# Five buffers instead of three for float64 weight blocks, loads four blocks ahead, and another choice of the blocks that are converted early

## The chip, the cores and the metric

The kernel runs on one core of one Trainium2 chip. The metric is the time of one execution in microseconds (us), the median of several runs; smaller is better. The engines are named as the profile names them: PE is TensorE (PEld its weight loads), DVE VectorE, ACT ScalarE, POOL GpSimd, and SP the engine whose queue issues every DMA of this kernel.

## What is computed

Sigmoid attention over 8 batches of 12 heads (448 tokens, head size 64), then a block that adds the real part of a two-dimensional Fourier transform, normalizes, and applies a feed-forward layer with a residual. All inputs are float32 but the two weight matrices, which are float64.

```python
def _attn_ref(q, k, v):
    scores = scale * np.matmul(q, k.transpose(0, 1, 3, 2)) - np.log(S)
    attn = 1.0 / (1.0 + np.exp(-scores))
    return np.matmul(attn, v).astype(np.float32)

def _moe_ref(x, w_ch1, w_ch2):
    X = np.fft.fft(np.fft.fft(x, axis=1), axis=2)
    u = x + np.real(X).astype(np.float32)
    mu = np.mean(u, axis=-1, keepdims=True)
    var = np.mean((u - mu) ** 2, axis=-1, keepdims=True)
    un = (u - mu) / np.sqrt(var + 1e-06)
    ch = np.maximum(un @ w_ch1, 0.0) @ w_ch2
    return (u + ch).astype(np.float32)
```

Here x is the output of attention, 3584 tokens of 768 numbers; w_ch1 is 768 x 3072 and w_ch2 3072 x 768.

## The kernel before

**Weights.** Each matrix is cut into 24 blocks, (0, f) of the first and (1, f) of the second, 128 partitions of 768 float64 words, 768 KB. Float64 words are handled as pairs of 32-bit integers. Three things happen to a block. Its largest magnitude is taken over the upper halves of its words (weight_max, L289: one DVE instruction, `wmax<-wr`); the scales of the matrices come out of all 48 maxima. It is converted to float32 (to_float32, L295: ACT at L300, DVE at L302, L306 and L308). And it is split into a high and a low float16 half with the scale (prep_w, L464: ACT at L491, DVE at L495).

**Attention** (L618 to L638) runs in steps t of one tile of scores: TQ = 168 steps, emitted in pairs. A pair emits what earlier pairs left for ACT and DVE (flush), the maxima that are due (`when_w`), the scores of two tiles (PE at L155 and L148, sigmoid on ACT at L159), the entries of the table `extra` for these steps, the loads that are due (`loads_w`), the products with v of two tiles LAG = 2 steps back (L176), and some units of the Fourier mixing of an earlier batch (mix_units, L208). Units write PSUM banks (`psd`, `pss`, `psx`), of which two are used at a time here; ACT or DVE reads a bank an emitted pair later (A, Q on ACT; sm, df and u on DVE, L240 and L259), and only then is it free for another unit. POOL casts queries and keys (L131), DVE makes their remainders ql and kl (L136).

The maximum of block n = 24 i + f stands at step 22 + n * 114 // 48, a block every 2.4 steps. Loads of blocks (weight_load, L282) go into three buffers called wr, and load n + 2 is emitted one step behind the maximum of block n, or two where block n - 1 is one of the set `ready`. The ten blocks of `ready` are converted as well (convert, L311) in three parts, at the step of the maximum and two and four steps behind it, into one of three buffers of float32 words (tag wt), and stored to t_dram (L318), 384 KB each. They are (0, 7), (0, 11), ... (0, 23) and (1, 5), (1, 9), ... (1, 21).

**Order.** `pin` (L529) binds every engine's instructions, SP's DMAs among them, to the order in which the code emits them, so an engine that waits holds up all that stands behind it.

**Towards the feed-forward.** The feed-forward takes blocks in the list `order`: (0, 0), (0, 1), (0, 2), (1, 0), (0, 3), (1, 1), (0, 4), (1, 2) and so on. Place k in it is a slot. prep_step (L498) emits a slot in four parts: loads of up to four places ahead, as far as buffers are free by `loadable`; the conversion on ACT of place k + 1 and the high half of place k - 1, whose float32 words are stored to t_dram; the conversion on DVE of place k; the low half of place k - 1. A block of `ready` is loaded from t_dram (L474), half as many bytes, and needs neither conversion nor store. Besides the three buffers wr two more, called spare, take the places from 8 on with k % 5 of 3 or 4.

A loop (L724 to L741) emits the last units of the mixing. It emits parts of slots too: of MIX_STEP rounds in turn the first four take one part each. Then come the chunks of 512 tokens. The first two are plain (NPLAIN): for each f an up-projection (PE at L669, result psh), its evacuation (evac, L672: hh on ACT, hl on DVE), two slots if the chunk is the first, and the down-projection of the f before (L688). The last five chunks run from a recombined copy of the weights, w_dram, with products in another form (L910, L961); the kept float16 blocks are written there from f = KEEP_FROM = 14 of the first chunk on (L784).

Of the kernel before, what the change touches and what calls it, by code (L numbers as in the profile page):

```python
# [11 lines left out]
I32 = mybir.dt.int32  # L12
# [11 lines left out]
DM = 768  # L24
# [3 lines left out]
NFC = DF // 128  # L28
# [4 lines left out]
BT = NT7 * NG  # L33
FOLDS = ((1, 2, 4, 5, 9, 9), (2, 2, 4, 4, 5, 5), (0, 0, 1, 1, 2, 2))
NPRE = 3
NW1 = 17
NW2 = 3
LEAD = 4
LNT = 2
UNIT_US = 0.66  # L40
MIX_UP = 8
MIX_STEP = 7

UN_SCALE = 1.0
TW = 512
# [15 lines left out]
def spectral_attention_ffn(tc, q, k, v, w1, w2, cd, cs, ident_in, out):  # L61
# [8 lines left out]
    with ExitStack() as top:  # L70
# [12 lines left out]
        wpre = top.enter_context(tc.tile_pool(name="wpre", bufs=1))  # L83
        w1p = wpre.tile([128, NPRE, 2, NCC, 128], F16, tag="w1p", name="w1p")
        w1h, w1l = [w1p[:, f, 0] for f in range(NPRE)], [w1p[:, f, 1] for f in range(NPRE)]
        w2h, w2l = [], []
# [3 lines left out]
        if True:  # L90
# [3 lines left out]
            io = att_ctx.enter_context(tc.tile_pool(name="io", bufs=2))  # L94
# [185 lines left out]
            wtile = {}  # L280

            def weight_load(n):  # L282
                if n < 2 * NFC:
                    i, f = divmod(n, NFC)
                    wtile[n] = t = wpre.tile([128, DM, 2], I32, tag="wr", name="wr", bufs=3)
                    nc.sync.dma_start(
                        t.rearrange("p n w -> p (n w)"), (w1, w2)[i][:, f * 2 * DM:(f + 1) * 2 * DM])

# [156 lines left out]

            prep = {}

            ready = {(i, f) for i in range(2) for f in range(7 - 2 * i, NFC, 4)}
            order = [(0, f) for f in range(NPRE)]
            for f in range(NFC):  # L450
                order += [(1, f)] + [(0, f + NPRE)] * (f + NPRE < NFC)

            spare = []

# [74 lines left out]
            def pin():  # L529

                ins = nc.cur_bb.bb.instructions
                for i in ins[seen[0]:]:
                    e = str(i.engine)
                    if e in seen[1]:
                        tc.add_manual_dep(
                            i, seen[1][e].name,
                            mybir.DependencyInfo(mybir.DependencyClass.NoSync, mybir.DependencyReason.DATA),
                            reason="order")
                    seen[1][e] = i
                seen[0] = len(ins)  # L540
# [18 lines left out]
            TQ = NT7 * GG  # L559
            TP = max(TQ - 4 * NPRE - 10, 1)  # L560
            TM = TP - 10
# [3 lines left out]
            loads_w = {}  # L565
            for t, x in when_w.items():
                for n in x:
                    loads_w.setdefault(t + (2 if divmod(n - 1, NFC) in ready else 1), []).append(n + 2)
            extra = {}

            def at(t, fn):
                extra.setdefault(t, []).append(fn)
# [24 lines left out]
                    at(4 + 4 * c + 2 * par, lambda c=c, par=par: nc.sync.dma_start(cd_sb[:, c, par], cd[:, c, par]))  # L597
            at(12, lambda: nc.sync.dma_start(cs_sb, cs))
            at(14, lambda: nc.sync.dma_start(ident, ident_in))
            at(16, lambda: weight_load(0))  # L600
            at(18, lambda: weight_load(1))
            nc.vector.memset(ones, 1.0)
            for n in range(5):
                at(TP - 8 + 2 * ((n + 1) // 2), lambda n=n: weight_scales(n))
            prepped = set()
            for e in range(NPRE + 2):
                for n, d in enumerate((-2, 2, 4, 6, 8, 10)):
                    t = TP + 4 * e + d
# [9 lines left out]
            for t in range(0, TQ + LAG + 4, 2):  # L618
                flush(sp_next)
                flush(act_next)  # L620
                flush(dve_next)
                for i in range(t, t + 2):
                    for n in when_w.get(i, ()):
                        weight_max(n)
                for i in range(t, t + 2):
                    if i < TQ:
                        scores(i)
                for i in range(t, t + 2):
                    for fn in extra.pop(i, ()):
                        fn()  # L630
                    for n in loads_w.get(i, ()):
                        weight_load(n)
                for i in range(t - LAG, t - LAG + 2):
                    if 0 <= i < TQ:
                        values(i)
                mix_some(2 * UNIT_US)
                pin()
# [5 lines left out]
        with ExitStack() as fast, ExitStack() as st, ExitStack() as early:  # L643
# [6 lines left out]
            def blocks(pool, i, fs):  # L650
                for f in fs:
                    t = pool.tile([128, 2, DM], F16, name=f"w{i + 1}_{f}")
                    both[i, f] = t
                    for n, x in enumerate(((w1h, w1l), (w2h, w2l))[i]):
                        x.append(t[:, n].rearrange("p (c f) -> p c f", f=128) if i == 0 else t[:, n])

            both = {(0, f): w1p[:, f].rearrange("p n c f -> p n (c f)") for f in range(NPRE)}
            blocks(wp, 0, range(NPRE, NW1))
            blocks(wp, 1, range(NW2))
# [64 lines left out]
            while units or act_next or dve_next or sp_next:  # L724
# [6 lines left out]
                if len(units) < MIX_UP and m < NCC:  # L731
                    up_proj(0, 1, range(m, m + 1))
                    m += 1
                n = step % MIX_STEP
                if n < 4 and slot < NPRE + 2 * NW2 and (n or len(units) > 3):
# [11 lines left out]
            ps_o = st.enter_context(tc.tile_pool(name="ps_o", bufs=1, space=PSUM, side="right"))  # L747
            blocks(wp2, 0, range(NW1, NFC))
            blocks(wp2, 1, range(NW2, NFC))
# [86 lines left out]
            for j in range(NFC):  # L836
                f = 1 + j - (j > 4) - (j > 8) - (j > 12) - (j > 16)
# [4 lines left out]
            for n, x in enumerate(kept):  # L842
                at = KEEP_FROM + n // 3 if n < 3 * (NFC - KEEP_FROM) else NFC + n - 3 * (NFC - KEEP_FROM)
# [6 lines left out]
            for c in range(NPLAIN):  # L850
                for f in range(NFC):
# [27 lines left out]
                    pin()  # L879
                    if c == NPLAIN - 1 and f == NW1 + 1:  # L880
                        early.close()
# [133 lines left out]
            for c in range(NPLAIN + 1, NCK):  # L1015
                t = (c - NPLAIN - 1) * NQ * NU
# [3 lines left out]
            for g in range(NGR):  # L1020
                t = g * NU
# [84 lines left out]
```

## Time and profile before

| | us |
|---|---|
| time before, median of 3 runs | 1670.48 (1667.25 to 1673.29) |
| the profiled execution's own time | 1672.77 |
| its span in the trace | 1670.9 |
| PE busy in it | 1621.0 (97%) |
| DVE busy | 1237.0 (74%) |
| ACT busy | 607.9 (36%) |
| POOL busy | 202.3 (12%) |

Attention ends at about 415 us of the span, the mixing loop at 440, the first plain chunk at about 635. The trace holds for every instruction its start, its duration and, where its engine sat idle before it, how long and whom it waited for. Durations of matmuls are modelled, so the starts tell more than the sums. A DMA's row on SP (SPq) is its issue, not its transfer. Groups of instructions read: line, engine, operation, output <- input, shapes, count, busy us, mean ns of one, idle us before them and what ended it.

### The profile page before, as it was taken

To read this page: it belongs to the slowest core of one execution; us is meant where nothing else is said; L and a number is where in the kernel's file an instruction comes from. 1 tells how busy PE (TensorE), PEld (TensorE's weight loads), DVE (VectorE), ACT (ScalarE), POOL (GpSimd) and SP (SyncE) were. 2 spreads that over 40 slices of the span, in tenths; PEclk is the share of its full clock that TensorE was granted. 3 is DMA by queue.
4 is the path that set the end of the run, shared out by engine and by line. 5 is a ranking of instruction groups with operands and counts; after the bars stand their busy time and mean duration, and the time that the engine had idled before them with its cause. 6 is when DMAs were issued, how large, how long until landed. Compare 5 with 4: busy or idle time off the path is not lost.

```text
span 1670.9 us, 27354 instructions
## 1 busy us (share of the span) xinstructions
PE 1621.0 (97%) x10913; PEld 1046.6 (63%) x10913; DVE 1237.0 (74%) x2393; ACT 607.9 (36%) x791; POOL 202.3 (12%) x219
## 2 busy tenths in 40 slices
PE   9989998999799999998999999999999999999997
PEld 4545454545455555554677777777777777777774
DVE  3456577767588756787568888888888888887777
ACT  5545454555254432333143323332333233323221
POOL 4535543455000000000000000000000000000000
PEclk9999999999899999999999999999999999999998
DMA  6665868756587985887675656565756565656561
GB/s 224 243 244 211 283 233 308 238 140 212 204 268 256 343 304 189 286 293 261 223 279 217 233 199 260 216 233 199 261 216 233 199 261 215 233 199 241 207 256 39
DMA packets 109185, 390.99 MB, mean 234 GB/s; under 512 B 22801, under 2 KB 48642, under 8 KB 93698
## 3 DMA queue, kind: packets, MB, share of 16 engines
q1 hardware_dynamic: 109058, 389.26, 64.9%
q8 instruction: 85, 1.39, 0.3%
q14 instruction: 42, 0.34, 0.1%
HBM read 312.15 MB, written 73.92 MB: 231 GB/s over the span
## 4 chain that ended last, share of the span: by engine, by line
PE 48%; DVE 2%; DMA 0%; ACT 0%; issue 0%; ACTq 0%; DVEq 0%
PE psf L910 24%; PE pso L961 23%; PE pst L808 1%; DVE acc L970 1%; DVE acc L985 0%; DMA ws<-w_dram 0%; DVE ur L989 0%; DVE F L916 0%; DVE H L916 0%; ACT H L945 0%; ACT F L935 0%; DVE X L916 0%; DVEq L916 0%; ACTq L945 0%; ACTq L935 0%
## 5 line engine op out<-in xcount | busy, mean ns | idle before, releaser
L961 PE MATMUL pso<-ws,H 128*128 128x384 f16 x2520 | 422.6, 326 | 0.9 <-DVE H L916 0.8
L910 PE MATMUL psf<-ut,ws 128*128 128x256 f16 x3780 | 422.1, 273 | 1.1 <-DVE ur L709 1.1
L910 PEld LDWEIGHTS <-ws 128*128 128x128 f16 x3780 | 369.8, 98 | 50.4 <-issue 1.4
L961 PEld LDWEIGHTS <-H 128*128 128x128 f16 x2520 | 246.4, 98 | 155.7 <-DVE H L916 1.1
L970 DVE TENSOR_TENSOR acc<-pso,acc 128x384 f32<-128x384 f32 x350 | 181.5, 548 | 19.1 <-PE pso L961 19.1
L159 ACT ACTIVATE a<-sc 128x900 f32<-128x900 f32 x168 | 147.6, 919 | 129.2 <-PE sc L155 112.7
L688 PE MATMUL po<-w,hh 128*128 128x512 f16 (+1 forms) x768 | 179.2, 328 | 7.3 <-ACT w L491 6.8
L935 ACT ACTIVATE F<-F 128x1024 f32<-128x1024 f32 x60 | 63.4, 1056 | 331.8 <-DVE F L916 331.8
L669 PE MATMUL psh<-ut,w 128*128 128x512 f16 x756 | 170.0, 379 | 2.0 <-ACT U L809 2.0
L916 DVE TENSOR_TENSOR H<-F,H 128x1024 f16<-128x1024 f32 x120 | 129.4, 1086 | 46.9 <-ACT H L945 46.9
L176 PE MATMUL av<-a,vr 128*64 128x450 f32 (+1 forms) x768 | 153.1, 568 | 0.0
L916 DVE TENSOR_TENSOR F<-X,psf 128x256 f32<-128x256 f32 x240 | 97.8, 417 | 51.5 <-PE psf L910 48.5
L945 ACT ACTIVATE H<-F 128x1792 f16<-128x1792 f32 x60 | 101.8, 1697 | 88.8 <-DVE F L916 88.8
L669 PEld LDWEIGHTS <-w 128*128 128x128 f16 x756 | 74.0, 98 | 91.4 <-issue 2.3
L688 PE MATMUL po<-w,hl 128*128 128x512 f16 (+1 forms) x384 | 126.1, 328 | 1.4 <-DVE hl L677 1.4
L688 PEld LDWEIGHTS <-hh 128*128 128x128 f16 x768 | 75.5, 98 | 56.3 <-issue 8.7
L916 DVE TENSOR_TENSOR F<-F 128x256 f32<-128x256 f32 x240 | 91.1, 421 | 17.2 <-ACT F L935 12.9
L291 DVE TENSOR_REDUCE wmax<-wr 128x1 f32<-128x768 f32 x48 | 45.5, 949 | 71.6 <-DMA wr<-w_in 71.6
L677 DVE SCALAR_TENSOR_TENSOR hl<-psh,hh 128x512 f16<-128x512 f32 x48 | 33.0, 687 | 80.6 <-ACT hh L676 80.6
L176 PEld LDWEIGHTS av<-a,vr 128*64 128x64 f32 (+1 forms) x768 | 39.5, 136 | 76.6 <-issue 73.6
L916 DVE TENSOR_TENSOR X<-X,psf 128x256 f32<-128x256 f32 x180 | 74.6, 414 | 16.5 <-PE psf L910 11.3
L218 PEld LDWEIGHTS psd<-cd_sb,xp 128*113 128x113 f32 x384 | 62.3, 180 | 25.1 <-issue 17.6
(108 smaller groups left out, 1748.4 us busy)
## 6 DMA issues: line engine op xcount, KB each, us to landing
ws<-w_dram SPq DMA_DIRECT2D x120, 1344.0 KB, 6.6
wr<-w_in SPq DMA_DIRECT2D x74, 768.0 KB, 7.4
cb<-t_dram SPq DMA_DIRECT2D x24, 768.0 KB, 5.3
t_dram<-wt SPq DMA_DIRECT2D x38, 384.0 KB, 5.9
qr<-q_in SPq DMA_DIRECT2D x48, 225.0 KB, 5.3
kr<-k_in SPq DMA_DIRECT2D x48, 224.0 KB, 6.4
vr<-v_in SPq DMA_DIRECT2D x24, 448.0 KB, 3.2
spare<-w_in SPq DMA_DIRECT2D x12, 768.0 KB, 5.6
```

The source lines that it names most:

```text
L159: nc.scalar.activation(a, ps[:, :, :SQ], AF.Sigmoid, bias=-math.log(S), scale=1.0 / math.sqrt(D))
L176: nc.tensor.matmul(avp[pr][j * D:(j + 1) * D, :SQ], vr[k, v0:v0 + D], a[k, j], start=(c == 3 * pr), stop=(c == 3 + 3 * pr))
L218: nc.tensor.matmul(ps[:HM, par * 193:par * 193 + 193], xp[:, kp ^ c, c, par, p], cd_sb[:, c, par, p], start=(p == par == 0), stop=(p == 2 ...
L291: nc.vector.tensor_reduce(out=wmax[:, i, f:f + 1], in_=wtile[n][:, :, 1].bitcast(F32), op=ALU.max, axis=AX.X, apply_absolute_value=True)
L669: nc.tensor.matmul(hs[c, f], l[f][:, m], r[:, m], start=(m == n == 0), stop=(m == NCC - 1 and n == 2))
L688: nc.tensor.matmul(po[n][:, at:at + hi - lo], l[:, cols], r[f][:, lo:hi], start=(f == 0 and m == 0 and at == 0), stop=(f == NFC - 1 and m ...
L910: nc.tensor.matmul(ps[:, :TH], w[:, x, a, m * 128:(m + 1) * 128], ut[y][:, b, m], start=(m == n == 0), stop=(m == n == 2))
L916: nc.vector.tensor_tensor(out=o, in0=x, in1=y, op=op)
L935: nc.scalar.activation(F[:, 0:4], F[:, 0:4], AF.Relu)
L945: nc.scalar.activation(hts[P][:, 0], F[:, 1:8], AF.Copy)
L961: nc.tensor.matmul(ps[:, :384], H[:, x, a, tp * 128:(tp + 1) * 128], w[:, y, b], start=(j == n == 0), stop=(j == 1 and n == 2))
L970: later(0, lambda: nc.vector.tensor_tensor(out=to, in0=ps[:, :384], in1=to, op=ALU.add))
```

## The change

Loads of float64 blocks during attention get two more buffers: block n uses one of the three wr buffers where n % 5 is 0, 1 or 2, and otherwise one of two buffers of the pool of attention's inputs, io, which is given back when attention ends. Load n + 4 stands where load n + 2 stood, and the first four go out at steps 16 to 19 in place of two at 16 and 18. The ten blocks that are converted in attention are now the places 3 to 12 of `order`: (1, 0), (0, 3), (1, 1), (0, 4), (1, 2), (0, 5), (1, 3), (0, 6), (1, 4), (0, 7). MIX_STEP goes from 7 to 4.

```diff
 NPRE = 3
+NREADY = 10
...
-MIX_STEP = 7
+MIX_STEP = 4
...
-                    wtile[n] = t = wpre.tile([128, DM, 2], I32, tag="wr", name="wr", bufs=3)
+                    wtile[n] = t = (io, wpre)[n % 5 < 3].tile(
+                        [128, DM, 2], I32, tag="wr", name="wr", bufs=2 + (n % 5 < 3))
...
-            ready = {(i, f) for i in range(2) for f in range(7 - 2 * i, NFC, 4)}
             order = [(0, f) for f in range(NPRE)]
             for f in range(NFC):
                 order += [(1, f)] + [(0, f + NPRE)] * (f + NPRE < NFC)
+
+            ready = set(order[NPRE:NPRE + NREADY])
...
-                    loads_w.setdefault(t + (2 if divmod(n - 1, NFC) in ready else 1), []).append(n + 2)
+                    loads_w.setdefault(t + (2 if divmod(n - 1, NFC) in ready else 1), []).append(n + 4)
...
-            at(16, lambda: weight_load(0))
-            at(18, lambda: weight_load(1))
+            for n in range(4):
+                at(16 + n, lambda n=n: weight_load(n))
```

Lines of the changed kernel are one to three higher. On SP, where the first blocks are loaded in attention (wr are blocks of weights, kr, qr and vr keys, queries and values), before:

```order
L286 DMA wr<-w_in 128x1536
L120 DMA kr<-k_in 128x448
L121 DMA qr<-q_in 128x450
L286 DMA wr<-w_in 128x1536
L120 DMA kr<-k_in 128x448
L121 DMA qr<-q_in 128x450
L127 DMA vr<-v_in 128x896
L286 DMA wr<-w_in 128x1536
```

and now:

```order
L288 DMA wr<-w_in 128x1536 x2
L121 DMA kr<-k_in 128x448
L122 DMA qr<-q_in 128x450
L288 DMA wr<-w_in 128x1536 x2
L121 DMA kr<-k_in 128x448
L122 DMA qr<-q_in 128x450
L128 DMA vr<-v_in 128x896
L288 DMA wr<-w_in 128x1536
```

Two more loads of blocks have gone out by the same key and query loads, and from there on each load is two blocks further ahead.

On DVE, in attention from step 80 on (u reads a bank of the mixing, ql and kl are remainders, a t with a number is a block's float32 words), before:

```order
L259 TENSOR_TENSOR u<-psx,df 113x384
L291 TENSOR_REDUCE wmax<-wr 128x1
L259 TENSOR_TENSOR u<-psx,sm 113x384 x2
L136 TENSOR_TENSOR ql<-qr,qh 128x450
L136 TENSOR_TENSOR kl<-kr,kh 128x384
L259 TENSOR_TENSOR u<-psx,df 113x384
L259 TENSOR_TENSOR u<-psx,df 112x384
```

and now:

```order
L260 TENSOR_TENSOR u<-psx,df 113x384
L293 TENSOR_REDUCE wmax<-wr 128x1
L308 SCALAR_TENSOR_TENSOR t_1802<-wr,t_1802 128x768
L310 SCALAR_TENSOR_TENSOR t_1802<-wr,t_1802 128x768
L304 TENSOR_SCALAR t_1846<-t_1846 128x768
L260 TENSOR_TENSOR u<-psx,sm 113x384 x2
L308 SCALAR_TENSOR_TENSOR t_1846<-wr,t_1846 128x768
L310 SCALAR_TENSOR_TENSOR t_1846<-wr,t_1846 128x768
L304 TENSOR_SCALAR t_1901<-t_1901 128x768
L137 TENSOR_TENSOR ql<-qr,qh 128x450
L137 TENSOR_TENSOR kl<-kr,kh 128x384
L260 TENSOR_TENSOR u<-psx,df 113x384
```

Six instructions of the conversions of (1, 0) to (1, 2) stand between reads of banks now; two more conversions follow in the next steps.

On ACT, from the evacuation of up-projection (0, 1) to that of (0, 2) (hh is the evacuation, w_0 to w_5 with a number are high halves, wt is a conversion), before:

```order
L676 ACTIVATE hh<-psh 128x512
L300 ACTIVATE wt<-wr 128x768
L491 ACTIVATE w_3_4086<-wt,wsc 128x768
L300 ACTIVATE wt<-wr 128x768
L491 ACTIVATE w_1_4101<-wt,wsc 128x768
L300 ACTIVATE wt<-spare 128x768
L491 ACTIVATE w_4_4087<-wt,wsc 128x768
L300 ACTIVATE wt<-spare 128x768
L491 ACTIVATE w_2_4102<-wt,wsc 128x768
L676 ACTIVATE hh<-psh 128x512
```

and now:

```order
L494 ACTIVATE w_3_4083<-wr,wsc 128x768
L494 ACTIVATE w_1_4098<-wr,wsc 128x768
L679 ACTIVATE hh<-psh 128x512
L494 ACTIVATE w_4_4084<-wr,wsc 128x768
L494 ACTIVATE w_2_4099<-wr,wsc 128x768
L494 ACTIVATE w_5_4085<-spare,wsc 128x768
L494 ACTIVATE w_3_4267<-spare,wsc 128x768
L679 ACTIVATE hh<-psh 128x512
```

The high halves of (0, 3) and (1, 1) (w_3_4083 and w_1_4098) have moved ahead of the evacuation, two more blocks are reached by the next, and no conversion stands among them.

## Prediction

> **What bounds the kernel now.** I read first the busy time by stage, then the waits of TensorE (PE), then the instructions of the engine that each of them names, and last the rows of the step at which the feed-forward begins. By stage (us; busy time of PE, its weight loads, DVE, ACT, POOL; granted clock, DMA share, GB/s):
>
> ```profile
> 0.00:440.00 440.00, 415.03 (x2512) 222.47 (x2513) 275.29 (x447) 218.97 (x294) 202.27 (x219) 0.98 0.67 228
> 440.00:464.00 24.00, 16.69 (x78) 8.15 (x77) 15.08 (x20) 8.44 (x11) 0.00 (x0) 0.79 0.81 276
> 464.00:560.00 96.00, 96.00 (x517) 50.30 (x515) 80.33 (x100) 46.89 (x60) 0.00 (x0) 1.00 0.81 268
> 560.00:608.00 48.00, 48.00 (x262) 25.54 (x261) 37.54 (x46) 21.99 (x28) 0.00 (x0) 1.00 0.94 341
> 840.00:1640.00 800.00, 799.15 (x6148) 602.82 (x6146) 652.59 (x1482) 245.09 (x325) 0.00 (x0) 1.00 0.60 225
> ```
>
> PE is the bound everywhere: full from 464 to 608 and, from 840 on, idle for 0.85 us in 800. The change touches only what lies before 608. There PE idles 440 - 415.03 = 25.0 us in attention and 24 - 16.69 = 7.3 us where the feed-forward begins, and the clock under 1.00 says that more is lost than the idle time. The largest stops in attention (start, duration, line, in brackets idle time before and whom PE waited for):
>
> ```profile
> 100.78 1.05 PE L252 MATMUL psx<-ident,xT 128*112 128x128 f32 x6 [3.62 <-DVE u L259]
> 104.34 0.74 PE L155 MATMUL sc<-qh,kl 64*128 64x450 f32 x2 [0.59 <-DVE kl L136]
> 200.07 1.05 PE L252 MATMUL psx<-ident,xT 128*113 128x128 f32 x6 [3.00 <-DVE u L259]
> 262.31 0.74 PE L155 MATMUL sc<-ql,kh 64*128 64x450 f32 x2 [6.07 <-DVE ql L136]
> 322.36 0.47 PE L155 MATMUL sc<-ql,kh 64*128 64x450 f32 x2 [2.17 <-DVE ql L136]
> ```
>
> They name DVE, but DVE was not busy: just before each it stood in order behind a maximum over a weight block that had not landed. The waits of DVE sum this up (total, times, longest):
>
> ```profile
> 98.04 0.95 DVE L291 TENSOR_REDUCE wmax<-wr 128x1 f32<-128x768 f32 x1 [6.13 <-DMA wr<-w_in]
> 198.60 0.95 DVE L291 TENSOR_REDUCE wmax<-wr 128x1 f32<-128x768 f32 x1 [5.26 <-DMA wr<-w_in]
> 260.76 0.95 DVE L291 TENSOR_REDUCE wmax<-wr 128x1 f32<-128x768 f32 x1 [6.50 <-DMA wr<-w_in]
> 315.05 0.95 DVE L291 TENSOR_REDUCE wmax<-wr 128x1 f32<-128x768 f32 x1 [1.73 <-DMA wr<-w_in]
> DVE wmax L291 <- DMA wr<-w_in: 71.6, 25, 8.1
> ```
>
> The second stop, where the feed-forward begins, is PE waiting for the high half of block (1,1), which ACT makes late because its conversion started late (below it SP's issues, a stretch of 8 us with its DMA rate at the end, and two rows of the page: KB each, median us to landing):
>
> ```profile
> 455.20 0.59 PE L688 MATMUL po<-w,hh 128*128 128x512 f16 x1 [6.84 <-ACT w L491]
> 456.26 0.58 PE L688 MATMUL po<-w,hh 128*128 128x512 f16 x1 [0.47 <-DVE w L495]
> 453.44 0.89 ACT L300 ACTIVATE wt<-wr 128x768 f32<-128x768 f32 x1 [10.61 <-DMA t_dram<-wt]
> 440.43 0.38 SPq L477 DMA_DIRECT2D wr<-w_in  x1
> 440.92 1.04 SPq L477 DMA_DIRECT2D spare<-w_in  x2
> 448.20 0.50 SPq L493 DMA_DIRECT2D t_dram<-wt  x1
> 448.00:456.00 8.00, 0.94 (x3) 0.18 (x2) 0.82 (x1) 1.71 (x2) 0.00 (x0) 0.65 0.97 389
> wr<-w_in SPq DMA_DIRECT2D x74, 768.0 KB, 7.4
> t_dram<-wt SPq DMA_DIRECT2D x38, 384.0 KB, 5.9
> ```
>
> Between the first and last of these issues the queue took five loads and three stores (768 and 384 KB each): 5.1 MB, which at the 389 GB/s of the stretch 448:456 takes 13 us, to 453.5. So the wait at 453.44 is a queue of bytes.
>
> **Attention: the longer lead.** Before, load n+2 is issued at step t(n)+1 or +2 and used at t(n+2), and blocks lie 2.4 steps apart: 2.8 to 3.8 steps of about 2.5 us (the stage has 168 steps), 7 to 9.4 us, against a landing of 7.4 us in the median. That is why 25 of 48 maxima wait. After, load n+4 goes out at the same step and has 4.8 steps more, 19 to 21 us; its buffer is that of n-1, whose last reader stands at t(n-1)+4, not after the load's step. Loads of 19 us lead and 7.4 us landing shouldn't wait, so the stops at 100.78, 262.31 and 322.36 go: 3.62 + 0.59 + 6.07 + 2.17 = 12.5 us. Each is followed by slow matmuls: eight value matmuls take 1.73 us before the stop at 262 and 3.06 after it.
>
> ```profile
> 251.77 1.73 PE L176 MATMUL av<-a,vr 128*64 128x450 f32 x8
> 263.44 3.06 PE L176 MATMUL av<-a,vr 128*64 128x450 f32 x8
> 323.23 2.37 PE L176 MATMUL av<-a,vr 128*64 128x450 f32 x8
> ```
>
> With the two pairs of score matmuls ahead of them (0.3 us each) that is 2.0 us after the stop of 6 us; I take 2 us for each of the three. Gain: 18.5 us. [...]
>
> **Attention: conversions in two clusters.** The ten conversions stay ten (one ACT and three DVE instructions and a store each), but move from every tenth step or so to steps 29-42 and 79-92, about 62-92 and 185-220 us. The costs by line, in attention and then at the feed-forward (busy, mean ns), and DVE's stretches:
>
> ```profile
> L308 DVE SCALAR_TENSOR_TENSOR t<-wr,t 128x768 int32<-128x768 int32 x10 | 12.3, 1232 | 0.3
> L306 DVE SCALAR_TENSOR_TENSOR t<-wr,t 128x768 int32<-128x768 int32 x10 | 11.4, 1139 | 0.0
> L302 DVE TENSOR_SCALAR t<-t 128x768 int32<-128x768 int32 x10 | 7.0, 703 | 3.4 <-ACT t L300 3.4
> L308 DVE SCALAR_TENSOR_TENSOR wt<-wr,wt 128x768 int32<-128x768 int32 x15 | 14.4, 958 | 0.5
> L302 DVE TENSOR_SCALAR wt<-wt 128x768 int32<-128x768 int32 x25 | 13.8, 551 | 0.0
> 62.00:92.00 30.00, 30.00 (x190) 15.49 (x190) 16.63 (x24) 16.57 (x23) 13.94 (x16) 1.00 0.50 177
> 193.00:220.00 27.00, 24.00 (x147) 13.84 (x149) 16.91 (x37) 11.15 (x15) 7.40 (x10) 0.94 0.88 326
> ```
>
> A conversion costs DVE 2.5 us (0.55 + 2 x 0.96) alone and 3.1 us (0.70 + 1.14 + 1.23) in attention. The first cluster adds four to 16.6 us of 30: 26.5 to 29, which fits. The second doesn't: five conversions less the one instruction that was there make 16.9 + 11.8 to 14.7 = 29 to 32 us of DVE work, where PE without its stop of 3.0 and its slow matmuls (about 1.6) needs 22.4. DVE is 6 to 9 us over. Part of it is slack (a remainder ql has three steps to its use, a bank of psx two transposes), so I expect PE to stop 4 to 6 us there in pieces, about what the stop at 200.07 costs today. The term is -1 us, from +4 (no stop left) to -5 (all 9 us felt). What queues behind the late DVE are the readers of the banks (L259), for whom PE's transposes wait; the stores of converted blocks hold SP's queue until DVE is done, and with it key and query loads, which go out six steps ahead of their first reader. [...]
>
> **Where the feed-forward begins.** The first ten blocks that it takes now come as float32 of 384 KB and need one ACT and one DVE instruction. The slots advance every 4 rounds of the mixing loop in place of 7, so two more blocks are done in it, and (1,1) stands ahead of the second evacuation on ACT and DVE. The five loads and three stores become three loads of 384 and two of 768 KB without stores, 2.8 MB or 7 us, and their users come an iteration later. The stop goes: 6.84 + 0.47, and the slow down-projection behind it:
>
> ```profile
> 440.41 0.59 PE L688 MATMUL po<-w,hh 128*128 128x512 f16 x2
> 444.31 4.05 PE L669 MATMUL psh<-ut,w1p 128*128 128x512 f16 x18
> 462.12 4.05 PE L669 MATMUL psh<-ut,w 128*128 128x512 f16 x18
> 434.69 0.59 PE L252 MATMUL psx<-ident,xT 128*113 128x128 f32 x3 [1.82 <-DVE df L240]
> 416.51 3.82 PE L218 MATMUL psd<-cd_sb,xp 128*113 128x193 f32 x22 [1.25 <-DVE u L259]
> ```
>
> From 440.41 to 444.31 one takes 3.90 us, from 455.20 to 462.12 less the 0.47 it takes 6.45, 2.55 too many. Together 9.9 us (bounds 8 and 10: what would be late next is the block after). In the mixing loop 4.4 us of conversions on DVE go (one L302, two each of L306 and L308), and three short instructions (L495, 1 us each) stand in place of one; of the 3.1 us in the last two rows I take 2 (0 to 3).
>
> **The plain stage after it pays.** The other 35 blocks in a row are now unconverted; before, nine among them were ready. Per iteration (7.78 us: an up-projection and a down-projection of 3.9 each) DVE has two blocks of 2.5 + 0.9 and the evacuation, 0.6: 7.4 us. It keeps up with 0.4 to spare, and DMA needs 2 x 1.15 MB in 7.78 us, 303 GB/s. In the last 48 us, where kept blocks are written too, the row 560:608 has 341 GB/s; two to four more full blocks there add 33 to 66: 374 to 407, about what the queue gave above (390). A lag of 4 us builds up at the end; an evacuation may be late by 7.78 - 1.3 = 6.5 us. So mostly hidden: I take -2 us (0 to -8, with slow matmuls after a stop).
>
> **Sum.** 18.5 - 1 + 2 + 9.9 - 2 = 27.4 us. The profiled execution took 1672.77 us (span 1670.9), the shown runs 1670.48 in the median; from the median that is **1643 us**.
>
> **Rivals.**
> - *All of DVE's lateness was the wait for loads* (0.12): the second cluster fits, the small waits go too. 18.5 + 4 + 3 + 10 = 35.5: 1635.
> - *DVE becomes the bound in the clusters* (0.18): all 9 us are felt, with clock losses, and some in the first. The gain in attention shrinks to 6, in all 16: 1655.
> - *The loads don't come sooner* (0.08). SP is in order, and a load can stand behind one of v that waits for its buffer (99.3 us in all, below). Its longest is 12 us, which 19 us of lead covers but for chance; else only the 12 us at the feed-forward stay: 1658.
>
> ```profile
> SPq L127 <- PE av L176: 99.3, 15, 12.0
> ```
>
> - *The plain stage becomes bound by its stores* (0.07), the one that could end slower. There are three buffers of float32 words; one is free when its store has landed. A block then takes a third of landing + 0.9 (ACT) + 2.5 (DVE): at 5.9 us 3.1, hidden under 3.89; at 8.3 it begins to cost, and over 35 blocks less 6.5 us of slack it eats 29.4 us when a block takes 4.9 us, that is when stores land after 11.3 us. Twice the median, with a queue at its limit only at the end: at a landing of 10.8, the longest now, 1664; at 12, 1678.
>
> **Chances.** Forecast 0.55, the others as given. A measurement of this kernel tells about 0.3% (5 us) from no change: faster 0.92, same 0.04, slower 0.04 (the last rival's two halves, with a little of the third). The range reaches from 3 us below the first rival to the third, 1632 to 1659; it leaves out the last, and an edge on either side.
>
> **What would show it.** Right: waits of DVE for wr under 15 us; no PE idle over 1 us near 100, 262 and 322; DVE over 0.9 busy from 185 to 215 with PE stops under 3 us each; no wait on L491 at the first down-projections; DVE over 0.9 busy from the third iteration to the twentieth, PE full. Wrong: a stop over 5 us in the second cluster, wr still waited for, or waits of ACT for stores of t_dram that reach PE after the fourteenth block.

## The result, and the profile after

The changed kernel takes 1643.72 us in the median of four runs (1641.55 to 1650.12), against 1670.45 us before (1667.25 to 1673.29): a ratio of 0.9847, with a 95% interval of [0.9812, 0.9882]. The profiled execution took 1645.79 us, with a span of 1643.8. One execution of one kernel further down ("no stores") took 2772.3 us at a granted clock of 0.556; its ratio leaves that execution out, and why it was slow is not known.

The same windows as before, of the kernel after (us; busy time of PE, its weight loads, DVE, ACT, POOL; granted clock, DMA share, GB/s):

```profile
0.00:440.00 440.00, 432.43 (x2664) 234.67 (x2665) 293.64 (x463) 230.54 (x309) 203.85 (x219) 1.00 0.71 245
440.00:464.00 24.00, 24.00 (x131) 12.61 (x129) 21.46 (x27) 12.21 (x17) 0.00 (x0) 1.00 0.85 267
464.00:560.00 96.00, 90.53 (x480) 45.97 (x477) 82.17 (x101) 44.04 (x56) 0.00 (x0) 1.00 0.96 314
560.00:608.00 48.00, 46.32 (x250) 24.15 (x250) 23.17 (x33) 10.44 (x14) 0.00 (x0) 1.00 0.70 250
```

PE's busy time and its granted clock say that the first window lost its stops and its slow clock (25.0 us of idle time to 7.6, 0.98 to 1.00), and that the third, full before, has 5.5 us of idle time now: the gain lies before 464 and a part of it is given back after. (The windows are fixed times, and the program is some 25 us further on in them.)

Time is compared better at the same instruction. Four instructions of PE divide the program: (a) the first psd behind attention's last value products, (b) the up-projection of f = 3, the first that reads a block from the pool w, (c) the first up-projection of the second chunk, (d) the last chain of pso. Before, at (c) and (d), then after, at (a) to (d):

```profile
625.77 4.05 PE L669 MATMUL psh<-ut,w1p 128*128 128x512 f16 x18
1639.27 20.64 PE L961 MATMUL pso<-ws,H 128*128 128x384 f16 x126
```

```profile
391.54 3.82 PE L219 MATMUL psd<-cd_sb,xp 128*113 128x193 f32 x22 [1.25 <-DVE u L260]
424.29 4.05 PE L672 MATMUL psh<-ut,w 128*128 128x512 f16 x18
596.74 4.05 PE L672 MATMUL psh<-ut,w1p 128*128 128x512 f16 x18
1612.13 20.64 PE L964 MATMUL pso<-ws,H 128*128 128x384 f16 x126
```

With the starts at (a) and (b) shown with the prediction, 416.51 and 462.12, each stretch follows by subtraction: attention 416.51 to 391.54; from (a) to (b), the mixing loop and the begin of the feed-forward, 45.61 to 32.75; the 21 iterations from (b) to (c), 163.65 to 172.45; the rest, 1013.50 to 1015.39. Gains of 25.0 and 12.9, losses of 8.8 and 1.9: 27.1 us.

The waits, after (total, times, longest), with the largest stops of PE left in attention and those new in the first plain chunk:

```profile
DVE wmax L293 <- DMA wr<-w_in: 8.1, 4, 4.5
ACT wt L302 <- DMA t_dram<-wt: 36.6, 12, 7.6
192.59 1.06 PE L253 MATMUL psx<-ident,xT 128*112 128x128 f32 x6 [0.48 <-DVE u L260]
198.34 0.59 PE L253 MATMUL psx<-ident,xT 128*112 128x128 f32 x3 [1.45 <-DVE u L260]
201.20 0.47 PE L156 MATMUL sc<-ql,kh 64*128 64x450 f32 x2 [0.47 <-DVE ql L137]
491.22 0.60 PE L691 MATMUL po<-w,hh 128*128 128x512 f16 x2 [0.61 <-ACT hh L679]
540.18 0.61 PE L691 MATMUL po<-w,hh 128*128 128x512 f16 x2 [1.12 <-ACT hh L679]
541.73 0.39 PE L691 MATMUL po<-w,hl 128*128 128x512 f16 x1 [0.95 <-DVE hl L680]
550.26 0.60 PE L691 MATMUL po<-w,hh 128*128 128x512 f16 x2 [1.00 <-ACT hh L679]
```

DVE waits 8 us for blocks in place of 72, and the stops of 3 to 6 us are gone. In the plain chunk PE now waits for evacuations, 7.1 us in nine stops between 491 and 570, where it had none: ACT reaches the evacuation late.

### The profile page after: what moved, and what is told of

Read it like the earlier page. It is cut to its first block, busy times and chain, and to the rows that moved or that the text cites. A ratio compares the mean times of both kernels' runs of the same rounds, so it can differ in the third digit from the quotient of the medians.

```text
span 1643.8 us, 27370 instructions
## 1 busy us (share of the span) xinstructions
PE 1611.1 (98%) x10913; PEld 1042.9 (63%) x10913; DVE 1242.4 (76%) x2393; ACT 607.5 (37%) x791; POOL 203.8 (12%) x219
## 4 chain that ended last, share of the span: by engine, by line
PE 49%; DVE 2%; ACT 1%; issue 0%; ACTq 0%; DVEq 0%
PE psf L913 24%; PE pso L964 24%; PE pst L811 1%; DVE acc L973 1%; DVE acc L988 0%; DVE F L919 0%; ACT H L948 0%; DVE ur L992 0%; DVE H L919 0%; ACT F L938 0%; DVE X L919 0%; ACTq L948 0%; DVEq L919 0%; ACTq L938 0%
## 5 line engine op out<-in xcount | busy, mean ns | idle before, releaser
L177 PE MATMUL av<-a,vr 128*64 128x450 f32 (+1 forms) x768 | 149.3, 558 | 0.0
L177 PEld LDWEIGHTS av<-a,vr 128*64 128x64 f32 (+1 forms) x768 | 38.8, 134 | 74.6 <-issue 70.5
L772 ACT ACTIVATE ch<-cb,wsc 128x1536 f16<-128x1536 f32 x24 | 37.8, 1576 | 102.7 <-DVE cb L768 97.1
```

What stands on the lines that cost most here:

```text
L177: nc.tensor.matmul(avp[pr][j * D:(j + 1) * D, :SQ], vr[k, v0:v0 + D], a[k, j], start=(c == 3 * pr), stop=(c == 3 + 3 * pr))
L772: nc.scalar.activation(h, t, AF.Copy, scale=wsc[:, i:i + 1])
```

## The experiments

In each, (a) to (d) are the four instructions above. Times in us; "all" is the median of the runs, with the ratio to runs of the kernel before on the same chip. Every kernel has 4 runs but the set alone (10) and the fourteen (5).

| kernel | to (a) | (a) to (b) | (b) to (c) | (c) to (d) | all | ratio, 95% interval |
|---|---|---|---|---|---|---|
| before | 416.51 | 45.61 | 163.65 | 1013.50 | 1670.45 | |
| after | 391.54 | 32.75 | 172.45 | 1015.39 | 1643.72 | 0.9847 [0.9812, 0.9882] |
| lead alone | 391.19 | 46.69 | 164.24 | 1015.00 | 1649.02 | 0.9868 [0.9841, 0.9896] |
| set alone | 419.96 | 34.80 | 169.63 | 1014.69 | 1672.42 | 1.0008 [0.9996, 1.002] |
| 7 rounds | 390.63 | 34.80 | 169.45 | 1014.97 | 1642.32 | 0.9834 [0.9811, 0.9857] |
| half the stores | 390.61 | 32.75 | 168.87 | 1013.26 | 1640.28 | 0.9822 [0.9803, 0.9841] |
| later writes | 390.92 | 34.42 | 170.53 | 1015.05 | 1640.48 | 0.9825 [0.9803, 0.9847] |
| less DVE | 391.56 | 32.75 | 163.49 | 1013.40 | 1636.11 | 0.9794 [0.9764, 0.9823] |
| no stores | 390.34 | 34.42 | 163.49 | 1013.29 | 1635.41 | 0.9784 [0.9753, 0.9815] |
| twenty-one | 398.91 | 32.75 | 163.48 | 1014.76 | 1642.93 | 0.9840 [0.9817, 0.9863] |
| five and six | 395.65 | 32.75 | 171.85 | 1014.82 | 1648.28 | 0.9866 [0.9846, 0.9886] |
| seventeen | 395.04 | 32.76 | 163.48 | 1017.16 | 1638.53 | 0.9803 [0.9771, 0.9834] |
| seventeen, 7 rounds | 393.89 | 34.80 | 163.49 | 1014.73 | 1638.61 | 0.9805 [0.9778, 0.9832] |
| fourteen | 391.08 | 32.75 | 163.49 | 1015.28 | 1636.08 | 0.9795 [0.9782, 0.9808] |

Two things for reading it. Where (a) to (b) is 34.4 or 34.8 rather than 32.75, 1.7 us of it is one chain of psd that takes 5.50 us in place of 3.82, in kernels of either pace (last section). And 163.49 in (b) to (c) is the stretch without any stop: 21 iterations of 7.785 us.

### Which part does what

**Lead alone** (short diff against the change):

```diff
-MIX_STEP = 4
+MIX_STEP = 7
-            ready = set(order[NPRE:NPRE + NREADY])
+            ready = {(i, f) for i in range(2) for f in range(7 - 2 * i, NFC, 4)}
```

> The lead alone: five buffers, loads four blocks ahead, four loads at the start; the set of ready blocks and the mixing loop's 7 rounds per block are those of before. Theory 'the lead is the whole of attention's gain': the end of attention (the last L216/L218 psd of before, at 416.51) comes 25 to 27 us sooner, waits of DVE for wr under 15 us; the stop of 6.8 us at the first down-projections stays, and so does the plain stage's length: 1670.5 - 26 = 1644 to 1646 us. Rival 'the place of the conversions made a part of it' (ten conversions spread out delay DVE ten times, two clusters only twice): attention's gain falls to the 15 to 18 us of the three large stops, 1652 to 1656 us.

Attention ends at 391.19, 25.3 us sooner, as the first theory said; the rival's 15 to 18 us are out. The stop at the first down-projections stays. In the kernel with the lead alone, DVE's wait for blocks, and the stops of PE at (a) and at the down-projection:

```profile
DVE wmax L293 <- DMA wr<-w_in: 6.6, 3, 4.6
391.19 5.50 PE L219 MATMUL psd<-cd_sb,xp 128*113 128x193 f32 x22 [1.26 <-DVE u L260]
431.54 0.58 PE L691 MATMUL po<-w,hh 128*128 128x512 f16 x1 [5.57 <-ACT w L494]
```

The total of 1649 is 3 us above the expected 1646: behind (a) the trace lost 1.1, 0.6 and 1.5 us in the three stretches, 1.7 of them the slow psd of the second row (5.50 us, after the change 3.82).

**Set alone**: the new set, with three buffers, loads two ahead, two loads at the start and 7 rounds, as before.

```diff
-                    wtile[n] = t = (io, wpre)[n % 5 < 3].tile(
-                        [128, DM, 2], I32, tag="wr", name="wr", bufs=2 + (n % 5 < 3))
+                    wtile[n] = t = wpre.tile([128, DM, 2], I32, tag="wr", name="wr", bufs=3)
...
-.append(n + 4)
+.append(n + 2)
...
-            for n in range(4):
-                at(16 + n, lambda n=n: weight_load(n))
+            at(16, lambda: weight_load(0))
+            at(18, lambda: weight_load(1))
```

> The set alone: the first ten blocks that the feed-forward takes are the ones converted in attention; three buffers, loads two ahead, two loads at the start, 7 rounds per block as before. Theory 'the set gives the stop where the feed-forward begins (10 us) and takes 9 to 11 us in the plain stage': attention within 3 us of before, the stop on the first down-projections gone, the rest of the first plain chunk 9 us longer: 1668 to 1674 us. Rival 'the clusters help attention too': attention 7 us shorter, 1661 to 1664 us. Rival 'clusters with three buffers hold up the loads': attention 5 to 10 us longer, 1675 to 1682 us.

1672.42, no change: 3.5 us lost in attention, 10.8 gained from (a) to (b), 6.0 lost from (b) to (c), and 1.2 after. That is the first theory by its total and its gain of 10 us; attention lies just outside its 3 us, and the plain stage lost less than its 9 to 11. In the kernel with the set alone DVE still waits for blocks, and PE's largest stops have only moved, each behind another maximum:

```profile
DVE wmax L292 <- DMA wr<-w_in: 65.3, 21, 6.6
229.84 0.74 PE L156 MATMUL sc<-ql,kh 64*128 64x450 f32 x2 [5.06 <-DVE ql L137]
277.04 3.24 PE L219 MATMUL psd<-cd_sb,xp 128*113 128x193 f32 x9 [5.35 <-DVE u L260]
```

So all of attention's gain is the lead's, and the set by itself gains at the begin of the feed-forward about what it loses elsewhere; on top of the lead, set and pace together are worth 5.3 us by the medians (1649.02 to 1643.72) and 5.0 by the spans of the two traces, though the intervals of the ratios overlap.

**7 rounds** of the mixing loop per block (`MIX_STEP = 7`), all else as changed:

> The change with 7 rounds of the mixing loop per block in place of 4. Theory 'the pace is worth nothing, since the loads and the float32 blocks are early enough': 1642 to 1647 us, no stop on the first down-projections. Rival 'the pace is what removed that stop': a wait of PE for ACT or DVE w of 3 to 7 us at 410 to 440 comes back, 1648 to 1655 us. Rival 'the faster pace moved conversions into the mixing loop and so is part of the plain stage's loss': 1 to 4 us sooner than the change.

1642.32: the pace is worth nothing that these runs can tell. In the trace (a) to (b) is 2.05 us longer, 1.7 of which are the chain of psd, and (b) to (c) 3.0 us shorter, which speaks for the third view: what the faster pace takes on in the mixing loop, it has to pay back behind it. No stop came back.

### What the plain stage lacks

The change loses 8.96 us between (b) and (c): 172.45 less 163.49.

**Half the stores** of the feed-forward's conversions left out, those of odd blocks from 9 on:

```diff
-                    if (i, f) not in ready:
+                    if (i, f) not in ready and not (f % 2 and f > 7):
                         nc.sync.dma_start(t_dram[i, f // 2][:, 1 - f % 2], t)
...
```

The second part of the edit, not printed, lets the later combinations of weights read the block that was stored in place of the one that was not.

> The change with the sixteen stores of the unconverted odd blocks from 9 on left out (the combinations of chunk 2's weights read the even block of such a pair twice, so those weights are not the reference's). It takes away landings that ACT waits for, and 6.3 MB of 55 or so from 425 to 640, and leaves DVE's work as it is. Theory 'three float32 buffers, each held until its store has landed': waits of ACT wt for t_dram fall by half or more, and the first plain chunk is 6 to 9 us shorter than in the change: 1635 to 1638 us. Theory 'DVE's rate, 7.4 of 7.78 us': it stays, 1642 to 1646 us.

Between the two: the loss is 5.4 in place of 8.96 us, and ACT's wait for stores 28.5 in place of 36.6. Neither forecast held.

**Later writes** of kept blocks (`KEEP_FROM = 16`):

> The change with the writes of kept blocks begun at iteration 16 in place of 14, so that they leave the queue free for two iterations more. Theory 'DMA at its limit once the kept blocks are written': the first stop of PE in the plain chunk (491 us, before either begins) stays and those from 540 on come later or are smaller, 2 to 5 us sooner: 1639 to 1642 us. Theories 'buffers' and 'DVE's rate': within 2 us of the change, 1642 to 1646 us.

The loss is 7.0 us, 1.9 less. The late stops did shrink to two, of 0.87 and 1.02 us at 560 and 569 (and two under 0.3), but stops of 0.4 to 0.6 came at 446 to 480, where this edit changes nothing. The runs' median is 3 us lower, the intervals overlap: a small share at most.

**Less DVE**: one of the three DVE instructions of a conversion left out in the feed-forward, so that the three lowest bits of those weights are missing.

```diff
...
-                    nc.vector.scalar_tensor_tensor(
+                    less or nc.vector.scalar_tensor_tensor(
                         out=ti, in0=lo, scalar=29, in1=ti, op0=ALU.logical_shift_right, op1=ALU.bitwise_or)
...
```

> The change with one of the three DVE instructions of a conversion in the feed-forward left out (the one that puts in the three lowest bits of the mantissa, so those weights differ in them), for the 35 blocks converted there: 0.96 us less of DVE each, all stores and transfers as in the change. Theory 'DVE's rate and its place between ACT's instructions': the 21 iterations take 164 to 167 us in place of 172.45, 1635 to 1639 us. Theory 'stores and buffers': a block then takes a third of the landing + 0.9 + 1.5, one microsecond in three less, and the rest of the landing shows as a wait of ACT for t_dram, which grows from 36.6 us; the 21 iterations take 169 to 172 us, 1641 to 1644 us.

**No stores** of conversions in the feed-forward at all (the later combinations, in a part not printed, read one stored pair for all):

```diff
-                    if (i, f) not in ready:
-                        nc.sync.dma_start(t_dram[i, f // 2][:, 1 - f % 2], t)
...
```

> The change with every store of a converted block in the feed-forward left out (38; the combinations read one stored pair of blocks for all, so chunk 2's weights are not the reference's): no float32 buffer waits for a landing, and 14.6 MB fewer go through the queue. Theory 'stores and buffers': the 21 iterations take 163.5 to 165 us in place of 172.45, 1634 to 1637 us. Theory 'DVE's rate': with half the stores left out they still took 168.87, and with none they take 167 to 169, 1638 to 1641 us.

Both take the whole loss away, to 163.49 us: each of the two theories is refuted by the other's experiment, if either is meant alone. The windows 452:500 and 500:548, of the change, of less DVE, and of no stores:

```profile
452.00:500.00 48.00, 46.83 (x253) 24.40 (x252) 41.80 (x52) 22.10 (x28) 0.00 (x0) 1.00 0.90 279
500.00:548.00 48.00, 45.93 (x247) 23.73 (x246) 41.01 (x51) 21.63 (x28) 0.00 (x0) 1.00 0.99 327
```

```profile
452.00:500.00 48.00, 48.00 (x263) 25.50 (x261) 35.49 (x46) 25.92 (x34) 0.00 (x0) 1.00 0.96 315
500.00:548.00 48.00, 48.00 (x261) 25.41 (x260) 30.15 (x39) 21.46 (x28) 0.00 (x0) 1.00 1.00 353
```

```profile
452.00:500.00 48.00, 48.00 (x262) 25.49 (x261) 45.21 (x56) 25.01 (x32) 0.00 (x0) 1.00 0.63 202
500.00:548.00 48.00, 48.00 (x260) 25.23 (x259) 45.17 (x57) 24.94 (x32) 0.00 (x0) 1.00 0.85 277
```

Without stores DVE works 45.2 of 48 us, 94%, and PE is full: DVE's rate is enough, as the prediction had it (7.4 of 7.78 us). With less for DVE, DMA is busy all the time (share 1.00, 353 GB/s, more than in the change), and PE is full too: that share by itself stopped nothing. What is too long in the change is the time for which one block holds one of the three float32 buffers, to which both contribute. One block in the change, by ACT's conversion, DVE's last instruction on it, SP's issue of its store, and ACT's conversion three blocks later, which takes over its buffer:

```profile
519.41 0.92 ACT L302 ACTIVATE wt<-wr 128x768 f32<-128x768 f32 x1 [1.51 <-DVE w L498]
524.70 0.96 DVE L310 SCALAR_TENSOR_TENSOR wt<-wr,wt 128x768 int32<-128x768 int32 x1
526.77 0.56 SPq L496 DMA_DIRECT2D t_dram<-wt  x1
534.91 0.91 ACT L302 ACTIVATE wt<-spare 128x768 f32<-128x768 f32 x1 [4.61 <-DMA t_dram<-wt]
```

This buffer is held for 15.5 us, one of the longest: 6.3 until DVE is done (its own 3.4 us of work on ACT and DVE, and the turns of the block ahead and of the evacuation in between), 1.1 to the store's issue, 8.1 to its landing (the median of all these stores is 6.2). At that, three buffers give a block every 5.2 us, and PE takes one every 3.89. This block and the six behind it hold their buffers for 13.1 to 15.9 us, 14.6 in the mean; the same seven conversions 13.7 with less DVE (the instruction left out takes 0.96), and 11.6 without stores, a third of which is 3.9. From 528.08 to 563.06 ACT converts seven blocks, one every 5.0 us:

```profile
528.08 0.92 ACT L302 ACTIVATE wt<-spare 128x768 f32<-128x768 f32 x1 [2.07 <-DMA t_dram<-wt]
...
563.06 0.92 ACT L302 ACTIVATE wt<-wr 128x768 f32<-128x768 f32 x1 [3.50 <-DMA t_dram<-wt]
```

and since ACT waits in order, the evacuation behind the waiting conversion is late, and PE stops. Without stores the same conversions come two in every 7.78 us, PE's own pace. With less DVE they don't keep it either. Its conversions at the same two places are these, seven blocks at 4.7 us each:

```profile
521.66 0.92 ACT L302 ACTIVATE wt<-spare 128x768 f32<-128x768 f32 x1 [1.92 <-DMA t_dram<-wt]
554.32 0.91 ACT L302 ACTIVATE wt<-wr 128x768 f32<-128x768 f32 x1 [2.70 <-DVE wt L310]
```

But it gets there 6.4 us sooner, at 521.66 in place of 528.08: in the 14 blocks before, which the change converts from 458 to 516 us, it took 3.83 us for one and the change 4.15. So the change loses its lead there, before its stores land slowest (8.1 us in the median of those issued from 516 to 566, 5.6 from 452 to 516), and with less DVE the lead covers the slow stretch. A fourth buffer, the direct test, was not tried.

### Where the conversions should stand

**Twenty-one** ready blocks: the ten, and every third of each matrix behind them (eleven more, where the expectation says ten):

```diff
-            ready = set(order[NPRE:NPRE + NREADY])
+            ready = set(order[NPRE:NPRE + NREADY]) | {(i, f) for i in range(2) for f in range(10 - 2 * i, NFC, 3)}
```

> The change with twenty blocks converted in attention in place of ten: the first ten and every third of each matrix after them, (1,8) to (1,23) and (0,10) to (0,22). Theory 'the plain stage loses 9 to 11 us since 35 unconverted blocks in a row overrun DVE, the stores or the DMA queue': at most two unconverted blocks then stand between ready ones on either matrix, the loss goes, and attention pays 0 to 3 us for 25 to 31 us more of DVE's work spread out: 1633 to 1637 us. Rival 'DVE's ten more conversions in attention are felt' (3 us each, half of them): the plain stage gains 10 and attention loses 10 to 15, 1643 to 1650 us. Rival 'the plain stage's loss is not from the unconverted blocks': its length stays, 1643 to 1647 us.

The plain stage is without a stop, but attention pays 7.4 us, between the first theory's 0 to 3 and the rival's 10 to 15, and the total is that of the change. PE's larger new stops (1.63 and 0.87 us near 238, 1.15 at 304) lie in and just behind the window 210:300, in which DVE goes from 70.5 us in the change to 79.0 of 90.

**Five and six**: `set(order[NPRE:NPRE + 5])` and (1, 8), (1, 14), (1, 20), (0, 10), (0, 16), (0, 22).

> The change with ten ready blocks of another choice: the first five that the feed-forward takes, and five later ones, (1,8), (1,14), (1,20), (0,10) and (0,16), (0,22) makes six on that rule. Theory 'the first few remove the stop, spread ones after them save the plain stage': the stop stays away, the plain stage's loss of 9 to 11 us is cut by a third to a half, attention as the change or 1 us worse: 1638 to 1642 us. Rival 'the stop needs all ten in a row': it comes back in part, 3 to 8 us between 410 and 470, and the sum is 1644 to 1650 us.

The rival: 1648.28, 4.6 us more than the change. The later stops are gone, but the conversions now begin right behind the mixing loop, and PE stops there for the evacuation (first row); attention pays 4.1 us around the blocks of the second matrix (second row). Rows of this kernel:

```profile
435.82 1.03 PE L691 MATMUL po<-w,hh 128*128 128x512 f16 x2 [3.37 <-ACT hh L679]
235.91 0.47 PE L156 MATMUL sc<-ql,kh 64*128 64x450 f32 x2 [1.60 <-DVE ql L137]
```

**Seventeen**: the ten and (0, 9), (0, 11) to (0, 21), whose maxima stand where DVE has room.

```diff
-            ready = set(order[NPRE:NPRE + NREADY])
+            ready = set(order[NPRE:NPRE + NREADY]) | {(0, f) for f in range(9, 23, 2)}
```

> The change with seven more blocks converted in attention, (0,9) to (0,21) by twos: their maxima stand between about 92 and 180 us, where the change leaves DVE 49 of 88 us busy, and in the plain stage every fourth block from the fourth unconverted one on is then ready. Theory 'where DVE has room, conversions are free, and one ready block in four keeps the plain stage full': the last value matmuls of attention start at 386 to 388 as in the change (386.32), the 21 iterations from the first up-projection of f = 3 to that of the next chunk take 163.5 to 166 us in place of 172.45: 1635 to 1639 us. Rival 'conversions cost PE wherever they stand' (0.7 us each, as the twenty did): attention 5 us longer, 1640 to 1643 us. Rival 'one in four is too few': the 21 iterations take 168 us or more, 1640 to 1644 us.

1638.53. The loss is gone, and attention pays 3.5 us, half a microsecond for each: theory and first rival each in part. The stretch (c) to (d), which the edit does not touch, happened to be 1.8 us longer in the profiled execution.

**Seventeen with 7 rounds:**

> The seventeen ready blocks with 7 rounds of the mixing loop per block in place of 4. Theory 'the pace only moves work between the mixing loop and the iterations after it': within 2 us of the seventeen at 4 rounds, the first down-projection 1 to 2 us later and the 21 iterations 1 to 3 us shorter if they still lose there. Rival 'the slower pace lets the first down-projections wait for their block again': 3 to 7 us slower than the seventeen at 4 rounds.

1638.61: within 0.1 us; the pace again tells nothing.

**Fourteen**: `range(11, 23, 3)` in place of `range(9, 23, 2)`, that is (0, 11), (0, 14), (0, 17), (0, 20).

> The change with four more blocks converted in attention, (0,11), (0,14), (0,17) and (0,20). The seventeen took the whole of the plain stage's loss away (163.48 us for the 21 iterations) and paid 3.5 us in attention (last value matmuls at 389.83 in place of 386.32), with stops at 101, 104, 139 and 152 us, the first two beside the conversion of (0,9). Theory 'each further conversion costs attention 0.5 us and a ready block in six is enough': last value matmuls at 387 to 388.5, the 21 iterations 163.5 to 166 us: 1636 to 1639 us. Rival 'one in six is too few': 168 us or more, 1640 to 1643 us. Rival 'only the place of (0,9) costs': 386.3 to 386.8 and 1634 to 1636 us.

1636.08 us, the lowest median of the kernels that compute everything, though its interval overlaps the seventeen's. Its interval [0.9782, 0.9808] lies below that of the change, [0.9812, 0.9882], each against runs of the kernel before on its own chip. Attention ends at 391.08, where the change ends it (391.54), so these four conversions between 92 and 180 us cost PE nothing, with room on DVE there (56.4 of 88 us busy, 49.3 in the change). In attention that is the rival named last; the total lies 0.1 us above its range. Of the seventeen's four stops there, at 101, 104, 139 and 152 us, the first two stood beside the conversion of (0, 9); which of the other blocks cost something was not tested. The plain stage is full, with ACT still waiting 26.4 us for stores. Rows of the kernel with fourteen, the window 92:180, the plain chunk, and that wait:

```profile
92.00:180.00 88.00, 87.34 (x543) 48.18 (x541) 56.37 (x76) 47.49 (x64) 42.48 (x49) 1.00 0.80 298
464.00:560.00 96.00, 96.00 (x517) 50.49 (x516) 79.02 (x97) 44.08 (x57) 0.00 (x0) 1.00 0.88 305
ACT wt L302 <- DMA t_dram<-wt: 26.4, 12, 8.3
```

A buffer still waits for its store here and there; that a ready block in every few gives ACT and DVE the time to catch up before PE notices is the likely reason, not one that a run isolates.

## Why the prediction came out right, and where its terms did not

The forecast was 1643 us and 27.4 us of gain; measured are 1643.7, and 27.1 in the trace. That it came out so close is luck: the gains in attention were forecast 7.4 us too small in sum, the losses behind them 8.7 us too small, and the two nearly cancelled.

| term | predicted | measured |
|---|---|---|
| stops in attention and slow matmuls behind them | 18.5 | 22.6 |
| second cluster of conversions | -1 (+4 to -5) | +2.3 |
| mixing loop | +2 (0 to 3) | +2.8 |
| stop where the feed-forward begins | +9.9 | +10.0 |
| rest of the first plain chunk | -2 (0 to -8) | -8.8 |
| second plain chunk and all behind | 0 | -1.9 |

The measured terms are differences of the gain at the same instruction of PE in both traces: at score matmuls between the stops 8.3 us by 184 us of the span before, 10.7 by 222, 20.2 by 297 and 25.0 by 335, then 27.8 at the first down-projection (440.41 before, 412.60 after), 37.8 at (b), 29.0 at (c), 27.1 at (d).

- **The cause of attention's stops** was right, and the experiments show it: the lead alone removes them, the set alone does not. Its size was read too small. The price of the slow clock was taken off the first value products behind each stop; behind the stop at 322 the chain after those was slow as well, by 1.0 us, as the two rows below show (20 matmuls of psd, before and after; the granted clock is 0.79 in 322:330 before, 1.00 in 298:306 after). Another 1.0 is a stop of 0.79 us at 144 that the sum left out. The other 2 us of the 4.1 were not traced.

```profile
325.53 4.52 PE L218 MATMUL psd<-cd_sb,xp 128*113 128x193 f32 x20
```

```profile
301.57 3.52 PE L219 MATMUL psd<-cd_sb,xp 128*113 128x193 f32 x20
```

- **The second cluster**: DVE's load there was estimated well, and what PE feels of it was not. DVE is full from 180 to 210 (first row, after), but PE's stops of 0.48, 1.45 and 0.47 us sum to 2.4 in place of 4 to 6: results may be later than I counted before PE stops. DVE's second OR took 1341 ns in attention (second row, after, up to 420 us), more than the 1232 from before. A conversion took 0.78 + 1.04 + 1.34 = 3.16 us there, so the upper figure of 3.1 came true, and the term of -5 that went with all 9 us felt did not.

```profile
180.00:210.00 30.00, 27.60 (x179) 15.57 (x177) 29.76 (x43) 15.72 (x21) 14.29 (x14) 1.00 0.70 252
L310 DVE SCALAR_TENSOR_TENSOR t<-wr,t 128x768 int32<-128x768 int32 x10 | 13.4, 1341 | 0.3
```

- **The mixing loop and the begin of the feed-forward** were right, in their mechanism and within 1 us (of the two stops shown for the mixing loop the 1.82 is gone, the 1.25 is in every kernel): the lead alone keeps the stop (5.57 us for ACT's w), the set alone loses it. That the pace has a part in it was wrong; with 7 rounds the stop stays away.

- **The plain stage** is the step that failed. It set three limits beside each other, DVE's 7.4 of 7.78 us, the queue's 374 to 407 GB/s, and the stores' "third of landing + 0.9 + 2.5", 3.1 us a block, and called the work hidden since each fitted. The last has the right form and the wrong terms: 0.9 + 2.5 is ACT's and DVE's work on a block, not the 6.3 us until it is done in their order, and 5.9 us the median landing before, with a DMA share of 0.81 from 464 to 560; from 516 to 566 after, at 0.96, the median is 8.1. 6.3 + 1.1 + 8.1 makes 15.5 in place of 9.3 us, and a third of it 5.2. The rival that was to cost 1664 us or more by stores that land after 10.8 us was this mechanism; it set in with landings of 8, and cost 9 us, not 30, since blocks came as slowly as one in 5.0 us only for seven of 35. Two of the prediction's own signs say the same: DVE was to be over 0.9 busy with PE full, and was busy 41.8 and 41.0 of 48 us with PE at 46.8 and 45.9; and of the signs of being wrong, the last, ACT's waits for stores that reach PE, did appear.

- **The -1.9 us behind it** is not explained. (c) to (d) varies from 1013.4 to 1017.2 us among kernels that are alike there.

- **The other rivals**: that all of DVE's lateness was the wait for loads came closest in attention (25.0 by the trace, near its 22.5); that DVE becomes the bound in the clusters, and that loads don't come sooner, are out, by PE's stops of 2.4 us and by the 8.1 us of waits for blocks.

## What to carry to other kernels

Where an engine in order waits for a transfer, move the transfer's issue ahead before moving the work: the rearrangement of conversions alone gained 10.8 us at the begin of the feed-forward and lost as much, 3.5 us of it in attention, where loads were still late. When work is moved out of a stage's slack, count how long a buffer is held from its first writer to the landing of its store, turns of other work included, and divide by the number of buffers; that each engine's rate and the queue's fit one by one does not say that their chain fits. Of a stage with a deficit, a few items taken away at regular distances can do as much as many at its head, if the stage that takes them has room just there.

## What the hardware did that was not expected

**Stops of 1.25 us left PE's granted clock at 1.00 in some kernels and at 0.79 in others.** The stop of 1.25 or 1.26 us at (a) is in all fourteen kernels, with the same instructions around it. The chain of psd behind it takes 3.82 us in eight of them, and 5.50 in the other six. Four of these six are among the five kernels with 7 rounds, so a part of the pace in it is not excluded; but it is 3.82 with 7 rounds before the change, and 5.50 with 4 rounds in two kernels. The windows 388:396 of the change and of the change with 7 rounds show the granted clock, 1.00 and 0.79 (the sixth figure behind the length of the window):

```profile
388.00:396.00 8.00, 6.42 (x40) 5.50 (x39) 3.71 (x7) 0.55 (x1) 3.91 (x3) 1.00 0.57 177
```

```profile
388.00:396.00 8.00, 6.42 (x29) 6.03 (x30) 3.41 (x7) 0.00 (x0) 3.73 (x3) 0.79 0.46 147
```

With the set alone a stop of 2.04 us left the next value products at their 1.73 us, where 2.17 us before the change made them 2.37:

```profile
212.81 0.47 PE L156 MATMUL sc<-ql,kh 64*128 64x450 f32 x2 [2.04 <-DVE ql L137]
213.28 0.47 PE L156 MATMUL sc<-qh,kl 64*128 64x450 f32 x2
213.68 1.73 PE L177 MATMUL av<-a,vr 128*64 128x450 f32 x8
```

Why stops alike in length differ in cost was not shown. The 1.25 us, with 0.3 us of idle time 2.3 us ahead of it, stood before 5.50 us of psd six times and before 3.82 eight times. Such a stop costs 1.7 us in some executions and nothing in others, so two traces that differ by that much in one stretch need not differ in their work.
